# Seven-product stage: sums of the weights on VectorE, squares on ScalarE, earlier splits, and separate slots for the last pair

## The chip, the cores and the metric

One core of one Trainium2 chip runs the whole kernel. The metric is device time in microseconds (us) of one launch, the median of several runs. Beside the timed runs there is one profiled execution of the same program, and all rows below come from that one. The engines are called PE (TensorE), DVE (VectorE), ACT (ScalarE), POOL (GpSimd) and SP (SyncE, which here issues transfers).

## The reference

Three steps follow one another: a retention layer over (4, 8, 576, 64), a feed-forward layer with a softmax-like gate and a layer norm, and a second feed-forward layer with a squared ReLU. The change touches the third one alone, for the last 1536 of the 2304 tokens:

```python
def _moe2_ref(x, w_in, w_out):        # x 2304 x 512, w_in 512 x 2048, w_out 2048 x 512
    h = x @ w_in
    r = np.maximum(h, 0.0)
    g = r * r
    return (g @ w_out).astype(np.float32)
```

All data is float32. Each matrix factor is held as a high part (rounded to the type that PE multiplies at full rate) and a low part (the rest), and a product is the sum of high x high, high x low and low x high.

## The kernel before

The order of every engine's instructions is the order in which the code issues them. The first two steps, and the second feed-forward layer for the first two blocks of 384 tokens, are issued from the string ORDER. The rest is `seven()`: three blocks of 512 tokens, eight *pairs* of weight units for each, so 24 pairs, numbered n = 0 to 23. A unit is 128 columns of w_in with the 128 rows of w_out that belong to them, and both stay on the chip.

In a pair, PE computes two first-layer tiles (`m3s(2n)` and `m3s(2n+1)`, 12 products of 512 columns each, L452 to L454), both into the one PSUM bank `acc["m"]`, so the second starts only when ACT has read the first (the ReLU of L527). The squares of the two tiles are a matrix of 2 x 2 sub-blocks A11, A12, A21, A22; the matching rows of w_out are B11, B12, B21, B22. Their 2 x 2 product is formed with seven products in place of eight. The left factors are A11, A12, A22, S4 = A12 - S2, S1 = A21 + A22, S2 = S1 - A11 and S3 = A11 - A21; the right ones are B11, B21, B22 and the sums T1 to T4 of the weights. `products(n, fs)` issues the six PE instructions of each product f (L540 to L542, 256 columns each), into seven PSUM accumulators p0 to p6 that live over a block.

The other engines prepare the factors:

- `sums(n)` (L553 to L559) forms T1 to T4 from both parts of the weights, on POOL, into the one buffer `sums`; in the first block T1 is formed too and overwrites B12 in its unit.
- `m3s` squares the ReLU's output on DVE (L528). `forms(n)` (L563) makes S1 to S4 on DVE.
- `split(f)` is `hi_lo`: ACT writes the high part (L85), DVE subtracts it for the low part (L86). `later_parts()` splits T2, T3, T4 in one operation of 768 columns and then A22, S1, S2 and S3. There is one slot for each split factor, so a split of pair n waits until the products of pair n-1 have read the slot.
- `xb_split` (L442 on ACT, L443 on POOL) splits the next block's input, one chunk in each of the last four pairs of a block.
- `result` (L596 to L608) adds p0 to p6 into the four output quarters at a block's end, spread over the next block's first two pairs; `result_last` does it at the very end.

On PE the order of pair n is `m3s(2n)`, products 0 to 2 of pair n-1, `m3s(2n+1)`, products 3 to 6 of pair n-1. On ACT and DVE, `later_parts()` of pair n-1 stands behind the ReLU and the square of `m3s(2n)`, and `sums(n)` is issued behind `forms(n)`. After the last pair, `later_parts()` and the seven products of pair 23 remain.

Of the kernel before, what the change touches and what calls it, by code (L numbers as in the profile page):

```python
# [9 lines left out]
F32R = mybir.dt.float32r  # L10
# [25 lines left out]
def tile_retention_solu_relu2(  # L36
# [23 lines left out]
    nc = tc.nc  # L60
# [435 lines left out]

    LEFT = ["A11", "A12", "S4", "A22", "S1", "S2", "S3"]
    RIGHT = ["B11", "B21", "B22", "T4", "T1", "T2", "T3"]
    sq, wf, part = {}, {}, {}

    def seven_tiles():
        a = x2p.tile([P, 2, 6, HS], F32R, tag="x2_0", name="parts")
        r_ = [dec.tile([P, 4, HS], F32R, tag="raw", name=f"sums{x}", bufs=3) for x in "hl"]
        for n, f in enumerate(LEFT[:6]):
            part[f] = (a[:, 0, n], a[:, 1, n])
        part["S3"] = (r_[0][:, 3], r_[1][:, 3])
        part["T"] = (r_[0][:, 0:3], r_[1][:, 0:3])
        for n, f in enumerate(("T3", "T4", "T2")):
            part[f] = (r_[0][:, n], r_[1][:, n])
        wf["f"] = dec.tile([P, 4, HS], F32, tag="raw", name="sums", bufs=3)  # L510
        acc["m"] = bank("h", [P, TS], "m3", 2)
        for n in (0, 1, 3, 4, 5):
            acc["p", n] = r_bank([P, 2, HS], f"p{n}")
        acc["p", 2] = bank("s", [P, 2, HS], "p2", 1)
        acc["p", 6] = bank("h", [P, 2, HS], "p6", 2)

    def factor(f, p):
        if f in part:
            return part[f]
        u, w = {"B11": (0, 0), "T1": (0, 1), "B21": (1, 0), "B22": (1, 1)}[f]  # L520
        return [x[:, 1, w * HS:(w + 1) * HS] for x in units[2 * p + u]]

    def m3s(i, then=lambda j: None):
        b, c = divmod(i, KF2)
        first_layer(acc["m"], NJOINT + b, c, then)
        g = bw["p"].tile([P, TS], F32, tag="g" if i % 3 == 2 else "rl", name="g", bufs=1 if i % 3 == 2 else 2)
        nc.scalar.activation(g, acc["m"], AF.Relu)  # L527
        nc.vector.tensor_tensor(g, g, g, ALU.mult)  # L528
        r = "1" if i % 2 == 0 else "2"
        sq["A1" + r], sq["A2" + r] = g[:, :HS], g[:, HS:]  # L530

    def products(n, fs):
        p = n % (KF2 // 2)
        for f in fs:
            lh, ll = part[LEFT[f]]
            rh, rl = factor(RIGHT[f], p)
            for t in range(2):
                w = slice(t * P, (t + 1) * P)
                o = acc["p", f][:, t]
                nc.tensor.matmul(o, lh[:, w], rh, start=(p == 0 and t == 0), stop=False, skip_group_check=True)  # L540
                nc.tensor.matmul(o, lh[:, w], rl, start=False, stop=False, skip_group_check=True)  # L541
                nc.tensor.matmul(o, ll[:, w], rh, start=False, stop=(p == KF2 // 2 - 1), skip_group_check=True)  # L542

    def split(f):
        hi_lo(*part[f], sq[f])


    def sums(n):
        p = n % (KF2 // 2)
        f = wf["f"]  # L550
        (h0, l0), (h1, l1) = units[2 * p], units[2 * p + 1]
        v = lambda x: x[:, 1].bitcast(F32).rearrange("q (a b) -> q a b", a=2)
        nc.gpsimd.tensor_tensor(f[:, 0::3], v(h0), v(l0), ALU.add)  # L553
        nc.gpsimd.tensor_tensor(f[:, 1:3], v(h1), v(l1), ALU.add)
        if n < KF2 // 2:
            nc.gpsimd.tensor_tensor(f[:, 3], f[:, 3], f[:, 0], ALU.subtract)
            hi_lo(*factor("T1", p), f[:, 3])
        nc.gpsimd.tensor_tensor(f[:, 2], f[:, 2], f[:, 3], ALU.subtract)
        nc.gpsimd.tensor_tensor(f[:, 0:2], f[:, 2:3].to_broadcast([P, 2, HS]), f[:, 0:2], ALU.subtract)  # L559

    def form(f, tag, x, y, op):
        sq[f] = bw["p"].tile([P, HS], F32, tag=tag, name=f, bufs=2)
# [2 lines left out]
    def forms(n):  # L565
        form("S1", "gh", "A21", "A22", ALU.add)
        form("S2", "gl", "S1", "A11", ALU.subtract)
        form("S4", "gh", "A12", "S2", ALU.subtract)
        split("A12")
        split("S4")  # L570
        form("S3", "gl", "A11", "A21", ALU.subtract)

    def later_parts():
        hi_lo(*part["T"], wf["f"][:, 0:3])
        for f in "A22", "S1", "S2", "S3":
            split(f)


    def res_out(r, c):
# [53 lines left out]
    def seven():  # L633
        np_ = KF2 // 2
        end = NSEV * np_
        for n in range(end):
# [3 lines left out]

            nxt = None
            if p >= np_ - KD and b + 1 < NJOINT + NSEV:
                nxt = lambda j: xb_split(b + 1, p - np_ + KD, nc.gpsimd) if j == KD - 1 else None
            m3s(2 * n, nxt or (lambda j: None))
            if n == 0:
                m4(NJOINT * KF2 - 1)
                sums(0)
            else:
                if p == 1 and n > 1:
                    result(b - 1, 2)  # L650
                later_parts()
                products(n - 1, range(0, 2) if n == end - 1 else range(0, 3))
                if p == 0:
                    result(b - 1, 0)
            split("A11")
            m3s(2 * n + 1)
            if n == end - 1:
                products(n - 1, range(2, 3))
            forms(n)
            if n:  # L660
                sums(n)
                products(n - 1, range(3, 7))
                if p == 0:
                    result(b - 1, 1)
        n = end - 1
        later_parts()
        products(n, range(0, 3))
        result(b, 0)
        for k in 5, 4, 6, 3:
# [119 lines left out]
```

## Time and profile before

| what | value |
|---|---|
| timed runs: median (lowest to highest of 3) | 740.79 us (739.29 to 741.36) |
| the profiled execution's own time | 744.68 us |
| its span, first to last instruction | 742.7 us |
| PE busy | 697.0 us, 94% |
| DVE busy | 589.6 us, 79% |
| ACT busy | 356.9 us, 48% |
| POOL busy | 281.7 us, 38% |
| mean granted clock of PE | 0.991 of full speed |

The seven-product stage is the last 288 us of the span: its first PE instruction starts at 454.42 us. Busy shares are means over stages with different limits, so the stage has to be read by itself, pair by pair. PE's matmuls are pipelined and their ends are modelled, so that the distance between two starts tells more of PE than the duration of one.

### The profile page before, as it was taken

The page shows a single profiled execution, that of the slowest core. Times are in us where ns is not written, and L with a number is a line of the kernel's source. Part 1 is how long each engine was busy: PE and PEld are TensorE (multiplying, and loading weights), DVE is VectorE, ACT ScalarE, POOL GpSimd, SP SyncE. Part 2 cuts the span into 40 slices and gives each one's busy share as a digit, 9 for nine tenths or more (in the row PEclk, how much of TensorE's full clock was granted, in tenths as well). Part 3 has the DMA queues.
Part 4 walks back from the last instruction along what each step waited for, and adds up shares of the span by engine and source line. Part 5 has one row for each costly group of instructions (what it writes and reads, how often), then busy time and mean ns, then how long its engine had stood idle before and what let it go on. Part 6 is the DMA issues. An engine that isn't in the chain of part 4 may idle for free. (4 is left out here: it accounts for less than half of the span.)

```text
span 742.7 us, 12712 instructions
## 1 busy us (share of the span) xinstructions
PE 697.0 (94%) x4928; PEld 620.4 (84%) x4928; DVE 589.6 (79%) x963; ACT 356.9 (48%) x761; POOL 281.7 (38%) x243
## 2 busy tenths in 40 slices
PE   0879999999999999999999999999999999999993
PEld 0768889888989999999989897987887988879993
DVE  4658998674656477548978886999999999999995
ACT  2656784563344454545646555433434344333342
POOL 3475664210212021013232324457662564534540
PEclk9999999999999999999999999999999999999998
DMA  9999991200000001012333303000002000020002
GB/s 198 192 225 225 204 227 60 71 2 0 30 1 30 1 29 33 26 57 88 112 94 105 113 30 85 2 1 1 1 1 57 1 1 2 1 57 1 1 1 57
DMA packets 66029, 44.97 MB, mean 61 GB/s; under 512 B 40497, under 2 KB 61105, under 8 KB 65969
## 3 DMA queue, kind: packets, MB, share of 16 engines
q1 hardware_dynamic: 65808, 44.03, 25.2%
q8 instruction: 38, 0.62, 0.4%
q14 instruction: 23, 0.18, 0.1%
q10 hardware_dynamic: 160, 0.13, 0.1%
HBM read 39.44 MB, written 4.72 MB: 59 GB/s over the span
## 5 line engine op out<-in xcount | busy, mean ns | idle before, releaser
L452 PE MATMUL m<-xh,uh 128*128 128x512 f32 (+1 forms) x320 | 118.8, 371 | 1.2 <-ACT g L527 0.7
L453 PE MATMUL m<-xl,uh 128*128 128x512 f32 (+1 forms) x320 | 118.2, 369 | 0.1
L454 PE MATMUL m<-xh,ul 128*128 128x512 f32 (+1 forms) x320 | 117.8, 368 | 0.0
L86 DVE TENSOR_TENSOR parts<-S,parts 128x256 fp32r<-128x256 f32 x72 | 78.6, 1118 | 5.0 <-ACT parts L85 4.8
L419 PE MATMUL m<-lh,woh 128*128 128x256 f32 x288 | 82.3, 286 | 0.0
L420 PE MATMUL m<-ll,woh 128*128 128x256 f32 x288 | 81.5, 283 | 0.0
L421 PE MATMUL m<-lh,wol 128*128 128x256 f32 x288 | 81.5, 283 | 0.0
L161 POOL TENSOR_TENSOR x<-x 128x512 int32<-128x512 int32 x24 | 36.1, 1503 | 112.5 <-DVE x L160 104.6
L85 ACT ACTIVATE parts<-g 128x256 fp32r<-128x256 f32 x72 | 29.6, 411 | 99.4 <-DVE g L528 99.4
L553 POOL TENSOR_TENSOR sums<-uh,ul 128x512 f32<-128x512 f32 x24 | 33.6, 1402 | 105.3 <-DVE sumsl L86 105.3
L452 PEld LDWEIGHTS m<-xh,uh 128*128 128x128 f32 x320 | 60.4, 189 | 9.5 <-ACT g L527 2.4
L454 PEld LDWEIGHTS m<-xh,ul 128*128 128x128 f32 x320 | 60.1, 188 | 7.8
L453 PEld LDWEIGHTS m<-xl,uh 128*128 128x128 f32 x320 | 60.3, 189 | 7.1 <-DVE xl L443 0.5
L542 PE MATMUL p<-uh,parts 128*128 128x256 f32 x192 | 56.1, 292 | 2.0 <-DVE parts L86 1.7
L356 PE MATMUL h<-wih,xh 128*128 128x512 f32 x144 | 57.7, 401 | 0.2 <-DVE e L379 0.2
L357 PE MATMUL h<-wil,xh 128*128 128x512 f32 x144 | 56.3, 391 | 0.0
L358 PE MATMUL h<-wih,xl 128*128 128x512 f32 x144 | 56.3, 391 | 0.0
L419 PEld LDWEIGHTS m<-lh,woh 128*128 128x128 f32 x288 | 55.2, 192 | 0.6 <-issue 0.2
L420 PEld LDWEIGHTS m<-ll,woh 128*128 128x128 f32 x288 | 55.2, 192 | 0.4
L421 PEld LDWEIGHTS m<-lh,wol 128*128 128x128 f32 x288 | 55.2, 192 | 0.0
L540 PE MATMUL p<-uh,parts 128*128 128x256 f32 x192 | 54.5, 284 | 0.3 <-ACT parts L85 0.3
L541 PE MATMUL p<-ul,parts 128*128 128x256 f32 x192 | 54.5, 284 | 0.0
(137 smaller groups left out, 1891.8 us busy)
## 6 DMA issues: line engine op xcount, KB each, us to landing
raw<-in_moe_w_out_dram SPq DMA_DIRECT2D x24, 512.0 KB, 3.4
raw<-in_moe_w_in_dram SPq DMA_DIRECT2D x20, 512.0 KB, 3.8
k<-in_k_dram SPq DMA_DIRECT2D x16, 256.0 KB, 6.7
q<-in_q_dram SPq DMA_DIRECT2D x16, 256.0 KB, 6.8
v<-in_v_dram SPq DMA_DIRECT2D x16, 256.0 KB, 6.8
out_dram<-x SPq DMA_DIRECT2D x32, 128.0 KB, 2.4
raw<-in_moe_w_in_dram SPq DMA_DIRECT2D x8, 256.0 KB, 7.7
q<-in_q_dram SPq DMA_DIRECT2D x4, 128.0 KB, 6.0
```

The source lines that it names most:

```text
L86: nc.vector.tensor_tensor(l, src, h.bitcast(F32), ALU.subtract)
L356: nc.tensor.matmul(p_, h_[:, i], wi_h[i][:, cols], start=(i == 0), stop=False)
L357: nc.tensor.matmul(p_, h_[:, i], wi_l[i][:, cols], start=False, stop=False)
L358: nc.tensor.matmul(p_, l_[:, i], wi_h[i][:, cols], start=False, stop=(i == KD - 1))
L419: nc.tensor.matmul(p_, wo_h[i][:, w], h_[:, i], start=(i == 0), stop=False)
L420: nc.tensor.matmul(p_, wo_h[i][:, w], l_[:, i], start=False, stop=False)
L421: nc.tensor.matmul(p_, wo_l[i][:, w], h_[:, i], start=False, stop=(i == KF - 1))
L452: nc.tensor.matmul(p_, uh[:, 0, w], xh, start=(j == 0), stop=False)
L453: nc.tensor.matmul(p_, uh[:, 0, w], xl, start=False, stop=False)
L454: nc.tensor.matmul(p_, ul[:, 0, w], xh, start=False, stop=(j == KD - 1))
L540: nc.tensor.matmul(o, lh[:, w], rh, start=(p == 0 and t == 0), stop=False, skip_group_check=True)
L542: nc.tensor.matmul(o, ll[:, w], rh, start=False, stop=(p == KF2 // 2 - 1), skip_group_check=True)
```

## The change

The sums of the weights move from POOL to DVE, and so does the subtraction of `xb_split` in this stage; POOL is left without an instruction there. The square moves from DVE to ACT (Square in place of the multiplication). The sums of pair n are issued ahead of A11's split instead of behind the forms, and the later splits of pair n are issued at the end of pair n, ahead of the next pair's ReLU, instead of behind it. The last pair gets slots of its own for T2 to T4, A22, S1, S2 and S3 (in the buffers of the input's splits, which are free by then), and its sums are split ahead of `m3s(47)`.

```diff
+    def last_slots():
+        for i, fs in enumerate((("T3", "T4"), ("T2", "A22"), ("S1", "S2"), ("S3",))):
+            x = [bw["p"].tile([P, 2, HS], F32R, tag=f"x{y}{i}", name="slots", bufs=2) for y in "hl"]
+            for n, f in enumerate(fs):
+                last[f] = tuple(y[:, n] for y in x)
+            if i == 0:
+                last["T"] = [(*x, slice(0, 2)), (None, None, slice(2, 3))]
+        last["T"][1] = (*last["T2"], 2)
+
+    def slots(n):
+        return last if n == NSEV * KF2 // 2 - 1 else part
...
         nc.scalar.activation(g, acc["m"], AF.Relu)
-        nc.vector.tensor_tensor(g, g, g, ALU.mult)
+        nc.scalar.activation(g, g, AF.Square)
...
-        nc.gpsimd.tensor_tensor(f[:, 0::3], v(h0), v(l0), ALU.add)
-        nc.gpsimd.tensor_tensor(f[:, 1:3], v(h1), v(l1), ALU.add)
+        nc.vector.tensor_tensor(f[:, 0::3], v(h0), v(l0), ALU.add)
+        nc.vector.tensor_tensor(f[:, 1:3], v(h1), v(l1), ALU.add)
         if n < KF2 // 2:
-            nc.gpsimd.tensor_tensor(f[:, 3], f[:, 3], f[:, 0], ALU.subtract)
+            nc.vector.tensor_tensor(f[:, 3], f[:, 3], f[:, 0], ALU.subtract)
             hi_lo(*factor("T1", p), f[:, 3])
-        nc.gpsimd.tensor_tensor(f[:, 2], f[:, 2], f[:, 3], ALU.subtract)
-        nc.gpsimd.tensor_tensor(f[:, 0:2], f[:, 2:3].to_broadcast([P, 2, HS]), f[:, 0:2], ALU.subtract)
+        nc.vector.tensor_tensor(f[:, 2], f[:, 2], f[:, 3], ALU.subtract)
+        nc.vector.tensor_tensor(f[:, 0:2], f[:, 2:3].to_broadcast([P, 2, HS]), f[:, 0:2], ALU.subtract)
...
-                nxt = lambda j: xb_split(b + 1, p - np_ + KD, nc.gpsimd) if j == KD - 1 else None
+                nxt = lambda j: xb_split(b + 1, p - np_ + KD, nc.vector) if j == KD - 1 else None
             m3s(2 * n, nxt or (lambda j: None))
             if n == 0:
                 m4(NJOINT * KF2 - 1)
-                sums(0)
             else:
                 if p == 1 and n > 1:
                     result(b - 1, 2)
-                later_parts()
                 products(n - 1, range(0, 2) if n == end - 1 else range(0, 3))
                 if p == 0:
                     result(b - 1, 0)
-            split("A11")
+            sums(n)
+            split(n, "A11")
+            if n == end - 1:
+                last_slots()
+                split_sums(n)
             m3s(2 * n + 1)
             if n == end - 1:
                 products(n - 1, range(2, 3))
             forms(n)
             if n:
-                sums(n)
                 products(n - 1, range(3, 7))
                 if p == 0:
                     result(b - 1, 1)
+            if n < end - 1:
+                split_sums(n)
+            later_parts(n)
         n = end - 1
-        later_parts()
         products(n, range(0, 3))
         result(b, 0)
```

PE's instructions and their order stay as they are. What moves stands on ACT and DVE, and the rows below show it for the middle of the stage, around pair 10 of 0 to 23. `g` is the buffer of a ReLU's output and its square, S1 to S4 are the forms, `sums` the weights' sums, `parts` and `sumsh`/`sumsl` the split slots; lines above L500 have other numbers in the changed file.

ACT before, from the ReLU of `m3s(21)` (L527) to that of `m3s(23)`:

```order
L527 ACTIVATE g_6104<-m3_5007 128x512
L85 ACTIVATE parts_5003<-g_6104 128x256
L85 ACTIVATE parts_5003<-S4_6111 128x256
L527 ACTIVATE g_6159<-m3_5007 128x512
L85 ACTIVATE sumsh_5004<-sums_5006 128x768
L85 ACTIVATE parts_5003<-g_6104 128x256
L85 ACTIVATE parts_5003<-S1_6107 128x256
L85 ACTIVATE parts_5003<-S2_6109 128x256
L85 ACTIVATE sumsh_5004<-S3_6117 128x256
L85 ACTIVATE parts_5003<-g_6159 128x256
L527 ACTIVATE g_6204<-m3_5007 128x512
```

The splits of pair 10's T, A22, S1, S2 and S3 stand behind the ReLU of `m3s(22)`, the second L527. ACT in the change, from the ReLU of `m3s(21)` (L539, with the square L540 behind it) to that of `m3s(22)`:

```order
L539 ACTIVATE g_6108<-m3_5007 128x512
L540 ACTIVATE g_6108<-g_6108 128x512
L85 ACTIVATE parts_5003<-g_6108 128x256
L85 ACTIVATE parts_5003<-S4_6115 128x256
L85 ACTIVATE sumsh_5004<-sums_5006 128x768
L85 ACTIVATE parts_5003<-g_6108 128x256
L85 ACTIVATE parts_5003<-S1_6111 128x256
L85 ACTIVATE parts_5003<-S2_6113 128x256
L85 ACTIVATE sumsh_5004<-S3_6121 128x256
L539 ACTIVATE g_6169<-m3_5007 128x512
L540 ACTIVATE g_6169<-g_6169 128x512
```

The same five splits now stand directly behind A12's and S4's, and the ReLU of `m3s(22)` and its square come after them. DVE in the change, pair 10 (L565 to L571 the sums, L86 the low parts, L575 the forms):

```order
L565 TENSOR_TENSOR sums_5006<-uh4_3781,ul4_3782 128x2x256
L566 TENSOR_TENSOR sums_5006<-uh5_3783,ul5_3784 128x512
L570 TENSOR_TENSOR sums_5006<-sums_5006 128x256
L571 TENSOR_TENSOR sums_5006<-sums_5006 128x512
L86 TENSOR_TENSOR parts_5003<-g_6069,parts_5003 128x256
L575 TENSOR_TENSOR S1_6111<-g_6069,g_6108 128x256
L575 TENSOR_TENSOR S2_6113<-S1_6111,g_6069 128x256
L575 TENSOR_TENSOR S4_6115<-g_6108,S2_6113 128x256
L86 TENSOR_TENSOR parts_5003<-g_6108,parts_5003 128x256
L86 TENSOR_TENSOR parts_5003<-S4_6115,parts_5003 128x256
L575 TENSOR_TENSOR S3_6121<-g_6069 128x256
L86 TENSOR_TENSOR sumsl_5005<-sums_5006,sumsh_5004 128x768
```

Four sums stand at the head of the pair, and no square (L528) is left; behind the last row come the four low parts of A22, S1, S2 and S3, and then pair 11's sums.

## Rows read from the trace of the kernel before

**Rows 1.** The page, part 1: busy time, share and instructions of each engine.

```profile
PE 697.0 (94%) x4928; PEld 620.4 (84%) x4928; DVE 589.6 (79%) x963; ACT 356.9 (48%) x761; POOL 281.7 (38%) x243
```

**Rows 2.** Waits, 480 to 742.7 us: waiter <- awaited: us in total, times, longest.

```profile
ACT parts L85 <- DVE g L528: 95.1, 24, 7.1
...
PE p L542 <- DVE parts L86: 5.6, 13, 0.8
```

**Rows 3.** Busy time by stretches cut at the first PE instruction of a pair.

```profile
core 0: us, PE busy (x) PEld busy (x) DVE busy (x) ACT busy (x) POOL busy (x), PEclk, DMA share, GB/s
454.42:463.17 8.75, 8.00 (x34) 5.85 (x32) 4.78 (x9) 4.87 (x10) 0.53 (x1) 1.00 0.71 156
...
507.76:519.98 12.22, 11.59 (x69) 9.80 (x68) 11.60 (x16) 5.11 (x13) 8.04 (x7) 1.00 0.01 1
...
555.52:570.01 14.49, 12.88 (x68) 10.88 (x67) 14.11 (x22) 4.29 (x10) 5.31 (x5) 0.88 0.35 74
570.01:580.53 10.52, 10.52 (x68) 9.54 (x67) 10.16 (x15) 4.30 (x10) 5.12 (x5) 1.00 0.00 0
...
646.53:661.30 14.77, 13.02 (x68) 10.88 (x67) 14.39 (x23) 4.34 (x10) 5.24 (x5) 0.89 0.34 71
...
714.02:733.06 19.04, 16.71 (x109) 14.71 (x108) 17.74 (x31) 8.06 (x19) 5.04 (x5) 1.00 0.00 0
473.80:714.02 240.22, 232.81 (x1389) 204.94 (x1388) 230.39 (x317) 97.61 (x233) 124.93 (x103) 0.99 0.05 10
```

**Rows 4.** Timeline of pair 10: start, us, engine, line, operation, out<-in.

```profile
572.35 0.42 DVE L86 TENSOR_TENSOR parts<-g,parts 128x256 fp32r<-128x256 f32 x1
...
572.76 0.28 PE L540 MATMUL p<-uh,parts 128*128 128x256 f32 x1
...
574.91 0.40 PE L452 MATMUL m<-xh,uh 128*128 128x512 f32 x1
...
575.42 1.41 POOL L553 TENSOR_TENSOR sums<-uh,ul 128x512 f32<-128x512 f32 x1 [5.25 <-DVE sumsl L86]
575.59 2.95 DVE L86 TENSOR_TENSOR parts<-S,parts 128x256 fp32r<-128x256 f32 x2
...
576.79 1.47 POOL L554 TENSOR_TENSOR sums<-uh,ul 128x512 f32<-128x512 f32 x1
...
577.66 0.28 PE L540 MATMUL p<-sumsh,parts 128*128 128x256 f32 x1
```

**Rows 5.** Groups by line and shape, 480 to 742.7 us: busy us, mean ns.

```profile
L86 DVE TENSOR_TENSOR parts<-S,parts 128x256 fp32r<-128x256 f32 x68 | 74.8, 1127 | 4.6 <-ACT parts L85 4.6
...
L528 DVE TENSOR_TENSOR g<-g 128x512 f32<-128x512 f32 x43 | 39.6, 922 | 3.2 <-ACT g L527 3.1
...
L85 ACT ACTIVATE parts<-g 128x256 fp32r<-128x256 f32 x66 | 27.1, 411 | 95.1 <-DVE g L528 95.1
...
L527 ACT ACTIVATE g<-m 128x512 f32<-128x512 f32 x43 | 25.5, 593 | 31.1 <-PE m L454 30.9
...
L563 DVE TENSOR_TENSOR S<-g 128x256 f32<-128x256 f32 x44 | 18.6, 422 | 0.8
...
L85 ACT ACTIVATE sumsh<-sums 128x768 fp32r<-128x768 f32 x22 | 18.4, 834 | 0.0
```

**Rows 6.** The same view, pair 10 alone (570.01 to 580.53 us): DVE's squares.

```profile
L528 DVE TENSOR_TENSOR g<-g 128x512 f32<-128x512 f32 x2 | 1.4, 682 | 0.0
```

**Rows 7.** Timeline, pair 9, the second pair of a block: first product 3 of PE.

```profile
564.25 0.36 PE L540 MATMUL p<-sumsh,parts 128*128 128x256 f32 x1 [0.93 <-DVE x L608]
```

**Rows 8.** Timeline of the end: a waiting product, and the output's first and last additions.

```profile
729.37 0.39 PE L540 MATMUL p<-sumsh,parts 128*128 128x256 f32 x1 [0.40 <-ACT parts L85]
...
731.42 0.69 DVE L617 TENSOR_TENSOR x<-x,p 128x512 f32<-128x512 f32 x1
...
735.13 0.75 DVE L630 TENSOR_TENSOR x<-x,p 128x256 f32<-128x256 f32 x2
```

**Rows 9.** Timeline of the stage's start: the first product of pair 1.

```profile
463.17 0.50 PE L452 MATMUL m<-xh,uh 128*128 128x512 f32 x1 [0.69 <-ACT g L527]
```

More of the change, by code (lines that the diff above doesn't have):

```diff
@@ L498, in tile_retention_solu_relu2 @@
     RIGHT = ["B11", "B21", "B22", "T4", "T1", "T2", "T3"]
-    sq, wf, part = {}, {}, {}
+    sq, wf, part, last = {}, {}, {}, {}
     def seven_tiles():
@@ L506, in seven_tiles @@
         part["S3"] = (r_[0][:, 3], r_[1][:, 3])
-        part["T"] = (r_[0][:, 0:3], r_[1][:, 0:3])
         for n, f in enumerate(("T3", "T4", "T2")):
             part[f] = (r_[0][:, n], r_[1][:, n])
+        part["T"] = [(r_[0][:, 0:3], r_[1][:, 0:3], slice(0, 3))]
+        last.update(part)
         wf["f"] = dec.tile([P, 4, HS], F32, tag="raw", name="sums", bufs=3)
@@ L515, in seven_tiles @@
         acc["p", 6] = bank("h", [P, 2, HS], "p6", 2)
+    def last_slots():
[8 more added lines that the diff above has]
+        return last if n == NSEV * KF2 // 2 - 1 else part
     def factor(f, p):
-        if f in part:
-            return part[f]
         u, w = {"B11": (0, 0), "T1": (0, 1), "B21": (1, 0), "B22": (1, 1)}[f]
@@ L534, in products @@
         for f in fs:
-            lh, ll = part[LEFT[f]]
-            rh, rl = factor(RIGHT[f], p)
+            lh, ll = slots(n)[LEFT[f]]
+            rh, rl = slots(n).get(RIGHT[f]) or factor(RIGHT[f], p)
             for t in range(2):
@@ L542, in products, with split @@
                 nc.tensor.matmul(o, ll[:, w], rh, start=False, stop=(p == KF2 // 2 - 1), skip_group_check=True)
-    def split(f):
-        hi_lo(*part[f], sq[f])
+    def split(n, f):
+        hi_lo(*slots(n)[f], sq[f])
     def sums(n):
@@ L568, in forms, with split_sums, later_parts @@
         form("S4", "gh", "A12", "S2", ALU.subtract)
-        split("A12")
-        split("S4")
+        split(n, "A12")
+        split(n, "S4")
         form("S3", "gl", "A11", "A21", ALU.subtract)
-    def later_parts():
-        hi_lo(*part["T"], wf["f"][:, 0:3])
+    def split_sums(n):
+        for h, l, w in slots(n)["T"]:
+            hi_lo(h, l, wf["f"][:, w])
+    def later_parts(n):
         for f in "A22", "S1", "S2", "S3":
-            split(f)
+            split(n, f)
     def res_out(r, c):
```

## The prediction
> **What bounds the kernel now.** The page comes first: PE is busy for 94% of the span, DVE for 79%, POOL for 38% [rows 1]. That says only that PE is nearly full as a mean, so the stage that the change touches is read by itself. The waits of that stage come next: ACT stood for 95.1 us until DVE had squared a tile, and PE stood 13 times until DVE had written a low part [rows 2]. ACT's 95 us cost nothing as such; the PE row is the one to follow, because it says that where PE waits, it waits for DVE.
>
> How much PE waits is read by cutting the stage into pairs [rows 3]. Pair 10 lasts 10.52 us and PE has no gap in it, so 10.52 us is what a pair costs when PE alone sets the time. Pair 5, with T1 and an input split on POOL beside the sums, lasts 12.22 us, and the second pair of a new block lasts 14.49 or 14.77 us at a granted clock of 0.88 and 0.89. Pairs 2 to 22, 21 of them, take 240.22 us, while 21 x 10.52 is 220.92 us. So **19.30 us** of those pairs is PE standing still or running at the lower of its two clock levels, 1.2 GHz, after it stood. The last stretch takes 19.04 us, where a pair and seven more products without a gap would take 15.54 (10.52, and 2.15 + 2.87 for the products, from the starts in [rows 4]).
>
> Then the question is why DVE is late. It is busy for 10.16 of the 10.52 us of even the clean pair [rows 3], but not with work of its own: a subtraction of 256 columns takes 0.42 us when POOL is idle, and two of them took 2.95 us from 575.59, while POOL ran two sums from 575.42 to 578.26 [rows 4]. Over the stage the same subtraction averages 1127 ns, 68 times, and the square 922 ns [rows 5], against 422 ns for a form of equal size [rows 5] and 682 ns for a square where POOL rests [rows 6]. **A DVE operation that meets POOL ends about when POOL's does.**
>
> **The change, part by part.** All durations are of the profiled execution. Its own time, 744.68 us, is 3.89 us above the median of 740.79; I take the difference that the change makes as the same in both.
>
> *POOL leaves, the sums go to DVE.* DVE gains four sums in a pair: three of 512 columns at 0.68 us (priced as the square that POOL did not meet [rows 6]) and one of 256 at 0.42, together 2.46 us. It loses two squares, 2 x 0.68 = 1.36. Its other work at the undisturbed price is four forms and seven low parts of 256 columns, 11 x 0.42 = 4.62, and one low part of 768, at most three times 0.42 = 1.26. Sum: 2.46 + 4.62 + 1.26 = 8.34 us in 10.52. In the first block T1 adds 0.84, and in eight pairs the input's split adds 0.84 (or 0.68): 10.02 at most. So DVE fits, tightly in pairs 4 to 7.
>
> *Squares on ACT.* No row shows a Square of 512 columns here. The nearest is the ReLU of the same tile on the same engine, 593 ns [rows 5]; from below it could be no less than the 411 ns of a 256-column copy, from above the 834 ns of a 768-column one. I take 0.60. ACT's pair is then four times 0.60, seven copies at 0.41 and one of 0.83, 6.1 us: it fits.
>
> *Does the new order make PE wait?* I walk one pair from its start at 0. From [rows 3, 4], PE does the even tile from 0 to 2.75, products 0 to 2 to 4.90, the odd tile to 7.65, products 3 to 6 to 10.52. ACT reads the odd tile from about 7.85 to 8.45 and squares it to 9.05. DVE makes S1, S2, S4 by 10.4, the low parts of A12 and S4 by 11.3, S3 by 11.7. ACT's split of T waits for product 6 (10.52), which read the slot; T, A22, S1, S2 and S3 take it from 10.85 to 13.3. The next even tile ends at 13.27 and its ReLU may start at 13.47: ACT is just free, and even 1.3 us later the odd tile at 15.42 would not notice. DVE's low parts end by 14.7, the sums by 17.15, A11 by 17.6; the next forms may start at 19.6. PE needs S4 at 14.7 and has it at 11.3; it needs T and A22 at 18.17 and has them by 13.4. **No wait is left in an ordinary pair**, with 1.3 us spare on ACT and 2.0 on DVE (0.3 in pairs 4 to 7). Gain: the 19.30 us above, less the next item.
>
> *Block ends.* The result's additions stay on DVE: one before the sums, three of about 0.69 behind S3 (priced as the one at 731.42 [rows 8]), four (two of 0.69, two in 0.75) ahead of the next pair's sums. By the same walk S3 is ready at 11.7, three additions 13.75, five low parts 16.7, the last addition 18.85. PE's product 3 overwrites what that addition reads, and wants to at 18.17. Rows show durations that overlap, so this wait lies between 0 and the 0.93 of before [rows 7]; I take 0.4 at each of two block ends: -0.8.
>
> *Start.* The stage's first 8.75 us hold 7.6 us of PE work; 0.69 of the rest is PE waiting for a ReLU with one bank [rows 9], which stays. About 0.45 goes with POOL. New is that in pair 1 five splits stand ahead of the ReLU without seven products before them: 0 to 0.7 us. Net +0.2, between -0.3 and +0.5.
>
> *End.* Now the last splits wait for product 6 of pair 22 and PE stands, at 729.37 for one [rows 8]. With own slots and the sums split before `m3s(47)`, the walk gives all low parts by 12.6 us after the pair's start, when product 5 needs S2 at 12.7. The addition that waits for product 5 can start at 10.52 + 2.15 + 0.72 + 0.2 = 13.6; before it started at 731.42 - 714.02 = 17.4. Behind it the chain of additions is the same, 731.42 to 735.88. Gain 3.8, between 2.5 and 4.2.
>
> **Sum:** 19.3 - 0.8 + 0.2 + 3.8 = 22.5 us. The span goes from 742.7 to 720.2, the profiled time to 722.2, the median to 740.79 - 22.5 = **718.3 us**. With every bound at its best the gain is 19.3 + 0.5 + 4.2 = 24.0, 716.8; the runs before lie up to 1.5 below their median, hence 715.3 as the lower end.
>
> **The rivals.** *Block ends keep their stall.* The additions come as late as before and PE stands, then runs at the lower level: pairs 9 and 17 keep their 3.97 and 4.25 us over 10.52. The gain falls by 8.2 - 0.8 to 15.1: 725.7 us. For it: my walk leaves nothing spare there. Against: pair 5 stood too, and the clock stayed at 1.00 [rows 3]; and DVE's backlog at these ends was POOL's. Chance 0.11.
>
> *ACT becomes the late one.* Five splits wait for product 6 and hold the next ReLU behind them, and the odd tile waits for that ReLU in the one bank. It decides when the splits end 1.3 us later than walked, say if S3 is late or Square costs the upper bound. At 0.3 us beyond that in each of 21 pairs: -6.3, 724.6 us. Chance 0.08.
>
> *DVE becomes the bound: slower.* If the stretching of DVE's operations did not come from POOL, the 10.16 us of the clean pair would stay, less 1.36, plus the sums at the stage's stretched ratio (922/682 x 2.46 = 3.33): 12.13, and 0.36 between operations as now, 12.49 us a pair. 21 pairs then take 262.3 instead of 240.2: 22.1 us more, 762.9. It turns from gain to loss at 240.22 / 21 = 11.44 us of DVE a pair. Against it: the same operation at 0.42 and 1.47 within four microseconds, told apart only by POOL [rows 4]. Chance 0.03. The Trainium skill's "Perfetto Trace Analysis" (Optimizing Scalar/DVE Operations) speaks for this side: where DVE is saturated, work should go off it, to ScalarE or even GpSimd; by that advice bringing sums to an engine at 97% loses, towards the 762.9. The same section adds that GpSimd shares an SBUF read port with DVE, so that moving work between those two may gain nothing; the trace agrees with this second half [rows 4], and that is why I do not follow the first.
>
> *Nothing comes of it.* PE is full in clean pairs, and if the waits of the others had another source than DVE's lateness, they would stay: 740 us. The main row of PE's waits names DVE [rows 2]. Chance 0.02.
>
> **How the numbers follow.** My forecast has the remaining 0.76. The range 715.3 to 727.0 takes in the two slower but still winning rivals and leaves out the last two and their mixtures. Faster by over 0.3% (2.2 us, about what this measurement can tell) are the first three cases, 0.95; same 0.02; slower 0.03.
>
> **What would show it.** Right: POOL has no row in the stage; DVE's low parts average near 0.42 us; pairs 2 to 22 last 10.5 to 10.6 us, but for pairs 9 and 17 at most a microsecond more; from the last pair's start to the first addition behind product 5 is about 13.6 us; the granted clock stays 1.00. Wrong: DVE's 256-column operations still far over 0.42 (slower), a ReLU that starts late behind S3's split (ACT), or pairs 9 and 17 near 14 us.

## The result, and the profile after

The changed kernel takes 719.96 us (median of four runs, 718.66 to 720.62) beside 740.04 us for the kernel before (739.16 to 741.36): a ratio of 0.9725, with a 95% interval of 0.9703 to 0.9748. That is 20.1 us less, where 22.5 were forecast, and the time lies inside the range of 715.3 to 727.0. The profiled execution took 720.62 us with a span of 718.9 us, 24.1 us under the profiled one of before.

The first view is the busy time by stretches, cut as in [rows 3]: pair 0, pairs 2 to 22 together, pairs 5, 9, 10, 17 and 20, and the last pair. The columns are those of [rows 3].

```profile
453.97:462.29 8.32, 7.64 (x34) 6.00 (x32) 4.58 (x10) 5.48 (x13) 0.00 (x0) 1.00 0.71 158
473.10:694.02 220.92, 220.92 (x1389) 200.31 (x1387) 171.17 (x377) 127.27 (x275) 0.00 (x0) 1.00 0.05 10
504.66:515.18 10.52, 10.52 (x68) 9.54 (x67) 8.64 (x21) 6.55 (x16) 0.00 (x0) 1.00 0.01 2
546.74:557.26 10.52, 10.52 (x69) 9.54 (x67) 10.20 (x22) 5.69 (x12) 0.00 (x0) 1.00 0.29 61
557.26:567.78 10.52, 10.52 (x69) 9.54 (x67) 8.09 (x19) 5.57 (x13) 0.00 (x0) 1.00 0.19 41
630.90:641.42 10.52, 10.52 (x69) 9.54 (x67) 10.20 (x22) 5.68 (x12) 0.00 (x0) 1.00 0.29 62
662.46:672.98 10.52, 10.52 (x69) 9.54 (x67) 7.30 (x17) 5.68 (x13) 0.00 (x0) 1.00 0.01 2
694.02:709.46 15.44, 15.44 (x110) 14.46 (x108) 12.96 (x29) 9.48 (x21) 0.00 (x0) 1.00 0.00 1
```

Read the length of each stretch first: from pair 2 to pair 22 every pair takes 10.52 us, the two at block ends (9 and 17) too, and 21 pairs take 220.92 us, which is 21 x 10.52 exactly. PE has no gap in any of them and the granted clock is 1.00 throughout. The fifth busy column, POOL's, is zero. DVE's, the third, is 171.17 / 21 = 8.15 us as the mean of these pairs, where before it was 230.39 / 21 = 10.97. In an ordinary pair without a block end (pair 20) it is 7.30, where the clean pair of before had 10.16 [rows 3], although DVE now does the sums and gave away only the squares.

The second view shows why: groups by line and shape, from 460 us on, to be set against [rows 5].

```profile
L540 ACT ACTIVATE g<-g 128x512 f32<-128x512 f32 x47 | 29.7, 632 | 1.5
L86 DVE TENSOR_TENSOR parts<-g,parts 128x256 fp32r<-128x256 f32 x71 | 29.7, 418 | 0.0
...
L86 DVE TENSOR_TENSOR parts<-S,parts 128x256 fp32r<-128x256 f32 x70 | 27.5, 420 | 3.7 <-ACT parts L85 1.1
...
L575 DVE TENSOR_TENSOR S<-g 128x256 f32<-128x256 f32 x48 | 20.3, 422 | 40.4 <-ACT g L540 40.4
...
L566 DVE TENSOR_TENSOR sums<-uh,ul 128x512 f32<-128x512 f32 x23 | 15.7, 683 | 0.0
```

The low parts that averaged 1127 ns now average 420. A sum on DVE takes 683 ns, as the square that POOL did not meet did [rows 6]; the square on ACT takes 632 ns. DVE now stands idle ahead of the forms, 40.4 us in all, until ACT has squared a tile. It was the engine that others waited for, and it waits now.

Five rows of the timeline carry the ends: PE's only wait in the whole stage (pair 1's start), the additions at pair 9 with the product that overwrites what they read, and the last additions.

```profile
462.29 0.50 PE L452 MATMUL m<-xh,uh 128*128 128x512 f32 x1 [0.69 <-ACT g L539]
...
553.31 0.75 DVE L623 TENSOR_TENSOR x<-x,p 128x256 f32<-128x256 f32 x2
...
554.39 0.28 PE L552 MATMUL p<-sumsh,parts 128*128 128x256 f32 x1
...
707.62 0.69 DVE L632 TENSOR_TENSOR x<-x,p 128x512 f32<-128x512 f32 x1 [0.59 <-PE p L554]
...
711.31 0.75 DVE L645 TENSOR_TENSOR x<-x,p 128x256 f32<-128x256 f32 x2
```

### The profile page after: what moved, and what is told of

It reads as the page before. It is cut to its first block, busy times and chain, and to the rows that moved or that the text cites. A ratio compares the mean times of both kernels' runs of the same rounds, so it can differ in the third digit from the quotient of the medians.

```text
span 718.9 us, 12609 instructions
## 1 busy us (share of the span) xinstructions
PE 686.3 (95%) x4928; PEld 618.1 (86%) x4928; DVE 522.9 (73%) x1032; ACT 390.9 (54%) x810; POOL 139.9 (19%) x127
## 4 chain that ended last, share of the span: by engine, by line
PE 90%; DMA 4%; DVE 3%; ACT 1%; issue 1%; SPq 0%; DVEq 0%; ACTq 0%
PE m L452 9%; PE m L453 9%; PE m L454 9%; PE p L554 6%; PE p L553 5%; PE p L552 5%; PE m L419 5%; PE m L421 5%; PE m L420 5%; PE h L356 4%; PE h L357 4%; PE h L358 4%; PE acc L482 3%; PE acc L483 3%; PE acc L481 3%; DMA raw<-in_moe_w_in_dram 3%
## 5 line engine op out<-in xcount | busy, mean ns | idle before, releaser
L539 ACT ACTIVATE g<-m 128x512 f32<-128x512 f32 x48 | 28.7, 598 | 64.7 <-PE m L454 64.5
L554 PE MATMUL p<-uh,parts 128*128 128x256 f32 x190 | 53.8, 283 | 0.0
L552 PE MATMUL p<-uh,parts 128*128 128x256 f32 x190 | 53.6, 282 | 0.0
L575 DVE TENSOR_TENSOR S<-g 128x256 f32<-128x256 f32 x48 | 20.3, 422 | 40.4 <-ACT g L540 40.4
L362 DVE TENSOR_REDUCE mx<-h 128x1 f32<-128x512 f32 x36 | 24.5, 687 | 31.3 <-PE h L358 31.0
```

## The experiments

The theory to test: a two-input operation of DVE is held while POOL runs one, so that POOL's sums made DVE late and DVE made PE wait. The rival: PE was freed by the sooner order of issue, and by the last pair's own slots. Each expectation below says what this means for its run, and so what its theory A, theory B or rival is. The runs' medians scatter by a few microseconds, and in the profiles of one and the same kernel most of this lies ahead of the stage (see the last section). So each kernel is also judged by its *stage*: from the first PE instruction of `m3s(0)` to the end of the span, in its profiled execution. The kernel before has 742.7 - 454.42 = 288.28 us, the changed one 718.9 - 453.97 = 264.93. Spans are shown to 0.1 us, so differences of stages are good to about 0.1 us.

| kernel | stage, us | against the changed one | median, us | ratio to before (95% interval) |
|---|---|---|---|---|
| before, first and second profile | 288.28, 287.67 | +23.4, +22.7 | | 1 |
| changed, three profiles | 264.93, 264.95, 265.01 | 0 | 719.96, 721.73, 719.27 | 0.9725 (0.9703 to 0.9748) |
| engines alone | 271.13 | +6.2 | 726.86 | 0.9774 (0.9727 to 0.9822) |
| order alone | 301.79 | +36.9 | 758.24 | 1.0193 (1.0141 to 1.0246) |
| sums on POOL | 272.96 | +8.0 | 727.92 | 0.9784 (0.9743 to 0.9825) |
| squares on DVE | 266.47 | +1.5 | 721.84 | 0.9711 (0.9666 to 0.9756) |
| idle work on POOL | 306.38 | +41.5 | 761.29 | 1.0245 (1.0228 to 1.0262) |
| shared slots at the end | 265.98 | +1.1 | 721.26 | 0.9693 (0.9670 to 0.9716) |
| stores on two queues, second bank | 263.23 | -1.7 | 719.33 | 0.9670 (0.9627 to 0.9712) |
| both ends | 262.56 | -2.4 | 717.48 | 0.9649 (0.9632 to 0.9665) |

Each ratio sets a kernel's runs beside runs of the kernel before taken with them. The changed kernel's is that of its first runs; its other two were 0.9703 and 0.9688. The first column has short names for the sections below.

### Engines alone

The kernel before with the change's engines alone; its order and its slots stay:

```diff
-        nc.vector.tensor_tensor(g, g, g, ALU.mult)
+        nc.scalar.activation(g, g, AF.Square)
...
-        nc.gpsimd.tensor_tensor(f[:, 0::3], v(h0), v(l0), ALU.add)
+        nc.vector.tensor_tensor(f[:, 0::3], v(h0), v(l0), ALU.add)
... (the other sums likewise)
-                nxt = lambda j: xb_split(b + 1, p - np_ + KD, nc.gpsimd) if j == KD - 1 else None
+                nxt = lambda j: xb_split(b + 1, p - np_ + KD, nc.vector) if j == KD - 1 else None
```

> The kernel before with the engines of the change alone: sums and input splits on DVE, squares on ACT, in the old order of issue and with the old shared slots at the end. Theory A (POOL stretches DVE's operations; with POOL silent DVE has 8.3 us of work in a pair of 10.52): DVE's 256-column low parts average 0.42 us, ordinary pairs last 10.5 us, pairs 4 to 7 at most 0.4 us more; the end keeps one to three of the 3.8 us, the block ends a microsecond or two; time 721 to 726 us. Theory B (the order of issue is what freed PE): the later splits still stand behind the ReLU and the sums behind the forms, so PE waits nearly as before and the time stays at 733 us or more.

Measured: 17.2 us of the 23.4 of the stage come with the engines alone, the time being just above the forecast span of theory A. The rows of the stretch from 480 us (within pair 2) to the end of pair 22, of the two block ends (pairs 9 and 17), and of the last pair:

```profile
480.00:697.83 217.83, 216.99 (x1356) 195.73 (x1355) 168.11 (x370) 123.31 (x271) 0.00 (x0) 1.00 0.05 11
548.46:560.10 11.64, 11.22 (x69) 9.59 (x67) 11.28 (x25) 5.73 (x13) 0.00 (x0) 1.00 0.32 68
633.74:645.23 11.49, 11.07 (x68) 9.58 (x67) 11.13 (x24) 5.72 (x13) 0.00 (x0) 1.00 0.33 71
697.83:718.92 21.09, 17.99 (x109) 16.59 (x108) 16.45 (x34) 9.02 (x20) 0.00 (x0) 0.87 0.00 1
```

PE is idle for 0.84 us in 218 us (two waits of 0.42 us, one at each block end). The block ends last 11.64 and 11.49 us, 2.1 us too many together; every other pair from 2 to 22 lasts 10.52. So ordinary pairs need nothing but the new division of engines. The last pair, though, takes 21.09 us to the last product, 2.05 more than before [rows 3] and 5.65 more than in the changed kernel. Its waits name one row:

```profile
PE p L540 <- ACT parts L85: 2.5, 1, 2.5
```

One product stood 2.5 us behind ACT's splits, and the clock of that stretch fell to 0.87. A silent POOL brings nothing at the end as long as sums and splits are issued late, as they are here.

### Order alone

The changed kernel with the old engines: the same lines as above, turned round.

```diff
-        nc.scalar.activation(g, g, AF.Square)
+        nc.vector.tensor_tensor(g, g, g, ALU.mult)
...
-        nc.vector.tensor_tensor(f[:, 0::3], v(h0), v(l0), ALU.add)
+        nc.gpsimd.tensor_tensor(f[:, 0::3], v(h0), v(l0), ALU.add)
... (the other sums likewise)
-                nxt = lambda j: xb_split(b + 1, p - np_ + KD, nc.vector) if j == KD - 1 else None
+                nxt = lambda j: xb_split(b + 1, p - np_ + KD, nc.gpsimd) if j == KD - 1 else None
```

> The changed kernel with the old engines: sums and input splits on POOL, squares on DVE, but the sooner order of sums and splits and the last pair's own slots. Theory A (POOL stretches DVE): DVE's low parts still average about 1 us, DVE is busy for 10 us of a pair, pairs 4 to 7 stay near 12 us; only the end gains 2 to 3 us; time 733 to 741 us. Theory B (the order is what freed PE): pairs fall to 10.6 us although DVE's operations are still stretched; time at most 725 us.

Measured: 758.24 us, slower than before and slower than either theory said. The order that belongs to the gain is a loss of 13.5 us of stage without the engines. The waits of the stage and the two pairs at the block ends (the columns are those of [rows 2] and [rows 3]):

```profile
PE p L552 <- DVE x L623: 11.6, 2, 5.8
...
PE m L452 <- ACT g L539: 10.1, 14, 1.8
```

```profile
559.70:578.34 18.64, 12.83 (x66) 11.39 (x67) 16.76 (x28) 5.02 (x12) 4.92 (x4) 0.82 0.25 52
578.34:588.84 10.50, 10.50 (x68) 9.53 (x67) 8.66 (x10) 3.99 (x9) 4.99 (x4) 1.00 0.05 10
654.66:673.58 18.92, 13.11 (x66) 11.67 (x67) 16.75 (x28) 5.02 (x12) 4.92 (x4) 0.82 0.26 54
```

These are two of the prediction's rivals, at work. Product 3 waited 5.8 us, twice, for the last addition of the result, which now stands behind five low parts that POOL stretches; each time the clock fell (0.82 in the stretch). And first-layer tiles waited 14 times for a ReLU, which now stands on ACT behind the five splits. The ordinary pair behind the block end is clean, 10.50 us, with POOL at work, while pairs 2 to 8 last 11.2 to 14.4 us: as before, what POOL costs it costs where DVE has little to spare. The last pair, with its own slots, takes 19.21 us from its first to its last product (727.03 to 746.24), where it took 19.04 before [rows 3].

### The weights' sums alone back on POOL

`sums(n)` as before, everything else as in the change:

```diff
-        nc.vector.tensor_tensor(f[:, 0::3], v(h0), v(l0), ALU.add)
+        nc.gpsimd.tensor_tensor(f[:, 0::3], v(h0), v(l0), ALU.add)
... (the other sums likewise)
```

> The changed kernel with the weights' sums alone back on POOL; squares stay on ACT, input splits on DVE, order and slots as in the change. DVE's own work is then 5.9 us in a pair, POOL's 5.1 (5.9 in the first block). Theory A in its strong form (any work of POOL in the stage makes PE wait): DVE is stretched by about 4 us a pair, the block ends stall again; time 728 us or more. Theory A in its weak form (POOL costs only where it meets DVE work that PE waits for): POOL runs in the gap in which DVE waits for the next odd tile's square, A11's low part and a few others are stretched, PE waits nowhere but perhaps at block ends; time 719 to 723 us.

Measured: 8.0 us more stage, between the two forms. The first block end (pair 9), the pair behind it and the second block end (pair 17):

```profile
544.68:557.78 13.10, 10.79 (x69) 9.46 (x68) 12.47 (x22) 6.10 (x13) 4.99 (x4) 1.00 0.22 47
557.78:568.30 10.52, 10.52 (x69) 9.54 (x68) 7.80 (x10) 5.38 (x12) 5.01 (x4) 1.00 0.21 43
631.42:646.01 14.59, 12.28 (x68) 10.95 (x67) 12.46 (x22) 6.09 (x13) 4.98 (x4) 0.88 0.30 63
```

The pair between takes 10.52 us with 5.01 us of POOL in it, and so does every pair from 2 to 22 but the block ends and pair 18 (10.49): the weak form holds there. The block ends take 13.10 and 14.59 us, 2.6 and 4.1 too many, because product 3 again waits for the last addition (4.6 us in two waits), and the second time the clock falls with it. So, once the squares are on ACT and the order is new, moving the sums to DVE is needed for the block ends and not for ordinary pairs. The rest is 0.8 us at the start (pair 2 starts 471.04 - 451.14 = 19.90 us after the stage's start, 19.13 in the changed kernel) and 0.6 us from pair 23's start to the end of the span.

### The squares alone back on DVE

```diff
-        nc.scalar.activation(g, g, AF.Square)
+        nc.vector.tensor_tensor(g, g, g, ALU.mult)
```

> The changed kernel with the squares alone back on DVE, POOL silent. DVE has 9.7 us of work in an ordinary pair of 10.52, 11.4 us in pairs 4 to 7. Theory A (DVE's own work is what counts once POOL is silent): ordinary pairs still last 10.52 us, pairs 4 to 7 run up a backlog of under 4 us that DVE's spare of about 3 us for the next products mostly takes, and the block ends, with 4.9 us of additions on top, stand for 1 to 3 us each; time 720 to 727 us. Rival (ACT's squares gave nothing, DVE has room): exactly the changed kernel's 720 us, no wait of PE at a block end.

Measured: 1.5 us more stage; by the medians no difference that can be told. The second row is a block end's:

```profile
451.93:718.40 266.47, 255.74 (x1594) 230.34 (x1592) 230.92 (x488) 117.85 (x274) 0.00 (x0) 0.99 0.08 19
544.88:556.02 11.14, 10.78 (x68) 9.45 (x67) 10.79 (x23) 4.00 (x9) 0.00 (x0) 1.00 0.26 55
```

A block end takes 0.62 us too many (11.14 - 10.52; the other 0.56), less than the 1 to 3 us of theory A, and pairs 4 to 7 take 10.52. With POOL silent, DVE had room for the squares, and this part of the change is worth 1.5 us of stage, 1.2 of it at the block ends. The parts do not add up: the sums alone put back cost 8.0 us and the squares alone 1.5, but sums, squares and the input's split together 36.9 (order alone). The input's split was not put back by itself.

### Work on POOL that nobody needs

Four additions on POOL in each pair from the third on, into a region that nothing reads; no other engine waits for their result:

```diff
+    def idle_work():
+        f = wf["f"]
+        for k in range(KD):
+            nc.gpsimd.tensor_tensor(x2[1][:, k, 0:TS].rearrange("p (a b) -> p a b", a=2), f[:, 0:2], f[:, 2:4], ALU.add)
...
             sums(n)
+            if n > 1:
+                idle_work()
             split(n, "A11")
```

> The changed kernel with four additions of 512 columns on POOL in each pair from the third on, behind the pair's sums: they read the sums' buffer and write a region that nothing reads, so no engine waits for their results. Theory A (POOL stretches DVE whether or not its result is needed): POOL's 5.6 us a pair fall on the forms and the low parts behind them, these average 0.8 to 1.4 us in place of 0.42, S3 gets late, the next ReLU behind it too, and pairs last 11 to 12 us: 735 to 750 us. Rival (DVE was late in the kernel before because it waited for POOL's results, not because its operations were held): DVE's operations keep 0.42 us and the time stays at 720 us.

Measured: 761.29 us, 41.5 us more stage, beyond the 750 of theory A; the rival falls. Groups by shape, then the timeline of one pair:

```profile
L576 POOL TENSOR_TENSOR x<-sums 128x512 f32<-128x512 f32 x78 | 109.7, 1435 | 160.5 <-DVE sums L571 160.5
...
L580 DVE TENSOR_TENSOR S<-S,g 128x256 f32<-128x256 f32 x21 | 28.4, 1352 | 0.7
```

```profile
589.22 0.42 DVE L86 TENSOR_TENSOR parts<-g,parts 128x256 fp32r<-128x256 f32 x1
589.44 5.65 POOL L576 TENSOR_TENSOR x<-sums 128x512 f32<-128x512 f32 x4 [5.70 <-DVE sums L571]
590.04 1.04 DVE L580 TENSOR_TENSOR S<-g 128x256 f32<-128x256 f32 x1 [0.40 <-ACT g L540]
591.11 1.40 DVE L580 TENSOR_TENSOR S<-S,g 128x256 f32<-128x256 f32 x1
592.55 1.40 DVE L580 TENSOR_TENSOR S<-g,S 128x256 f32<-128x256 f32 x1
593.86 1.51 DVE L86 TENSOR_TENSOR parts<-g,parts 128x256 fp32r<-128x256 f32 x1
...
595.30 0.41 DVE L86 TENSOR_TENSOR parts<-S,parts 128x256 fp32r<-128x256 f32 x1
```

POOL's four additions run without a break from 589.44 to 595.09, and in that time DVE gets four operations done, one for each. Ahead of it and behind it the same kinds take 0.42 and 0.41 us. No engine waits for these additions, so this is no wait for data: **while POOL runs two-input operations one after the other, DVE gets one operation in for each of them, if it reads both its inputs from SBUF** (the on-chip memory of the tiles; PE's accumulators lie in PSUM). In 21 of the 22 pairs with this work, four operations of DVE start during POOL's four. The condition is shown by the run with the sums on POOL, at its first block end:

```profile
551.81 0.96 DVE L86 TENSOR_TENSOR sumsl<-S,sumsh 128x256 fp32r<-128x256 f32 x1
552.57 1.34 POOL L571 TENSOR_TENSOR sums<-sums 128x512 f32<-128x512 f32 x1
552.69 0.67 DVE L619 TENSOR_TENSOR x<-x,p 128x512 f32<-128x512 f32 x1
553.29 0.67 DVE L620 TENSOR_TENSOR x<-x,p 128x512 f32<-128x512 f32 x1
```

The low part, of 256 columns, took 0.96 us, where it takes 0.42 with a silent POOL; POOL ran a sum then too (from 551.68 to 552.49 us). The two additions of the result, of 512 columns each, read one input from PSUM (`p`). They took 0.67 us each beside a single operation of POOL, where with a silent POOL they take 0.68. The mechanism was forecast, with too wide a condition and too low a price. A reason for the price that fits the rows, though it was not tried by itself, is that the held operations are the forms: ACT's splits stood for 91.6 us until forms were ready, where in the changed kernel it was 24.9, and through the splits PE's products and the next ReLU came late.

### Shared slots at the end

The changed kernel without `last_slots`, its sums split at the usual place:

```diff
-        return last if n == NSEV * KF2 // 2 - 1 else part
+        return part
...
-                last_slots()
-                split_sums(n)
+                pass
...
-            if n < end - 1:
-                split_sums(n)
+            split_sums(n)
```

> The changed kernel without the last pair's own slots: its later splits wait for product 6 of pair 22 in the shared slots, its sums are split at the usual place. Theory A (3.8 us of the gain belong to the last pair's slots): 2.5 to 4.5 us more, the last product 3.5 us later, with one or more waits of PE behind the splits and the lower clock level after them. Rival (the end's gain came from POOL's silence, the slots hide what is hidden anyway): under 1 us more.

Measured: about 1 us more stage (265.98 beside 264.93), so theory A's number falls, and the rival's limit of 1 us lies within the reading. One wait of PE is left, 0.54 us, and no fall of the clock:

```profile
705.09 0.39 PE L554 MATMUL p<-sumsh,parts 128*128 128x256 f32 x1 [0.54 <-DVE parts L86]
```

But the rival's reason falls too. From the last pair's first to its last product there are 19.04 us before, 21.09 with the engines alone, 16.22 here and 15.44 with the whole change. Engines alone and this run both have a silent POOL and shared slots; what differs is the order, so the sooner order is worth 4.9 us there. POOL need not be silent for it, as the last pair's rows of order alone, of the sums on POOL and of the squares on DVE show:

```profile
727.03:746.24 19.21, 16.63 (x107) 14.77 (x108) 17.56 (x31) 8.14 (x20) 4.98 (x4) 1.00 0.00 0
698.58:714.45 15.87, 15.70 (x110) 14.52 (x108) 14.29 (x25) 9.14 (x21) 5.00 (x4) 1.00 0.00 0
693.34:708.78 15.44, 15.44 (x109) 14.46 (x108) 14.12 (x32) 8.06 (x19) 0.00 (x0) 1.00 0.00 1
```

All three have the sooner order and the own slots. Among them the gain is lost only where POOL's sums and DVE's squares come together (19.21 us, DVE busy for 17.56 of them); the sums on POOL alone leave 15.87. The slots add the last microsecond.

### The stage's two ends

Two edits at first: the last stores half from ACT's queue, and the stage's second first-layer tile in product 6's bank.

```diff
-                store(b, 0, t)
+                store(b, 0, t, eng=(nc.sync, nc.scalar)[t])
...
-                store(b, 1, t, slice(1, 2))
+                store(b, 1, t, slice(1, 2), (nc.sync, nc.scalar)[t])
...
-        first_layer(acc["m"], NJOINT + b, c, then)
+        m = acc["p", 6].rearrange("q a b -> q (a b)") if i == 1 else acc["m"]
+        first_layer(m, NJOINT + b, c, then)
...
-        nc.scalar.activation(g, acc["m"], AF.Relu)
+        nc.scalar.activation(g, m, AF.Relu)
```

> The changed kernel with two edits at the stage's two ends: the last stores are issued half from SP and half from ACT (six each, where SP issued ten), and the second first-layer tile of the stage goes into the bank that product 6 uses later, so that the third need not wait for the second one's ReLU. If the tail is SP's issuing (10 issues in 6.4 us behind the first addition, then 2.5 us to land), it gets 2 to 3 us shorter, and the start 0.7 us: 716 to 718 us beside 720. If the tail is the transfers' own time, nothing but the 0.7 us.

Measured: 1.7 us less stage. The stores did that (from pair 23's start to the end of the span 24.9 us became 23.2); the bank did nothing (pair 2 starts 19.15 us after the stage's start, 19.13 in the changed kernel), since the next tile now waited longer for the next ReLU, which stands behind pair 0's five splits:

```profile
468.18 0.50 PE L452 MATMUL m<-xh,uh 128*128 128x512 f32 x1 [0.89 <-ACT g L540]
```

The third edit puts these splits, for pair 0 alone, behind that ReLU:

```diff
+                if n == 1:
+                    split_sums(0)
+                    later_parts(0)
                 products(n - 1, range(0, 2) if n == end - 1 else range(0, 3))
...
-            if n < end - 1:
+            if 0 < n < end - 1:
                 split_sums(n)
-            later_parts(n)
+            if n:
+                later_parts(n)
```

> The changed kernel with the last stores on two queues, the stage's second first-layer tile in product 6's bank, and, for pair 0 alone, the later splits behind the next ReLU instead of ahead of it. Before this third edit the wait of 0.69 us only moved: from the ReLU of the second tile to that of the third, which stood behind the five splits (0.89 us). If ACT's order is what the third waits for, both waits go now, and the stage is 1 us shorter than with two edits and 2.7 us shorter than the changed kernel's 264.9; if the splits are then late for the products behind, PE waits there instead and nothing is gained.

> The changed kernel beside the one with both ends edited, on the same chip: 719 to 723 us, its stage 264.9 us in the profile whatever the time ahead of it is.

Measured: 2.4 us less stage than the changed kernel, where 2.7 were expected: pair 2, behind the splits that moved, takes 10.95 us. The median is 717.48 us beside 719.27 on the same chip. The ratios to before, 0.9649 (0.9632 to 0.9665) and 0.9688 (0.9666 to 0.9710), are barely apart. Of PE's waits in the stage one of 0.3 us, of a weight load, is left. The stores' issue, in the timeline of the changed kernel and of this one:

```profile
709.92 6.40 SPq L603 DMA_DIRECT2D out_dram<-x  x10
```

```profile
708.66 4.46 SPq L604 DMA_DIRECT2D out_dram<-x  x6
708.66 4.75 ACTq L604 DMA_DIRECT2D out_dram<-x  x6
```

Ten issues in a row from SP lasted to 716.32, 4.3 us beyond the last addition; six from each queue last to 713.41, 2.6 us beyond it (its last addition ends at 710.81). By its stage this is the shortest version; by the medians its lead over the changed kernel is barely clear.

## Why the prediction was right, point by point

| term | forecast | measured in the profiled executions |
|---|---|---|
| pairs 2 to 22 | -19.3 | 240.22 to 220.92: -19.30 |
| block ends, part of those pairs | +0.8 | 0 |
| start, to the first instruction of pair 2 | -0.2 | 473.80 - 454.42 = 19.38 to 473.10 - 453.97 = 19.13: -0.25 |
| end, from pair 23's start to the last addition | -3.8 | 735.88 - 714.02 = 21.86 to 712.06 - 694.02 = 18.04: -3.8 |
| sum | -22.5 | the stage -23.4; the span -23.8, of which 0.45 lies ahead of the stage |

**What bounds the kernel** was read rightly: the clean pair's 10.52 us is what PE needs, and all else was waiting. **DVE's load** was forecast at 8.34 us for an ordinary pair, which was too much: pair 20 shows 7.30. Its 16 operations add up to 8.07 us, since the low part of 768 columns takes 0.96 us and not 1.26, and independent operations overlap (two low parts of 0.42 us start at 664.52 and 664.86).

**The cause** was read rightly, and shown directly by the idle work on POOL. The rule in bold, that a DVE operation which meets POOL ends about when POOL's does, was too wide: it holds for operations with both inputs in SBUF, not for the result's additions (0.67 us beside POOL's 1.34).

The Trainium skill's "Perfetto Trace Analysis" (Optimizing Scalar/DVE Operations) says that GpSimd and DVE share an SBUF read port. The held operations agree with that. It adds that offloading between those two "might not help"; here, the other way round, bringing the sums from POOL to DVE gained 8.0 us of stage. It also says that it may make sense to take work off a saturated DVE, to ScalarE or even GpSimd. The squares moved to ScalarE gained 1.5 us with a silent POOL, so that part agrees; the sums left on GpSimd would have kept the 8.0 us in the kernel.

**The block ends** were mis-sized, 0.8 us instead of none. The walk put the last addition's end at 18.85 us after the pair's start and PE's product 3 at 18.17; measured from 536.22, pair 8's start, they are 17.84 (553.31 + 0.75) and 18.17 (554.39). The walk added durations, and DVE's independent operations start sooner than that: the additions of 0.68 us start 0.60 apart (552.00 and 552.60, profile of the changed kernel). 0.33 us were spare. The runs with the sums on POOL and with the squares on DVE show how little that is: both stand here first.

**The start** came out by both its parts: pair 0 is 0.43 us shorter without POOL (8.75 to 8.32), and pair 1, with five splits ahead of its ReLU, 0.18 longer (10.63 to 10.81).

**The end** came out as forecast, its first addition at 707.62 - 694.02 = 13.6 us after the pair's start. Where the prediction put that gain was only half right. It named the slots and the early sums; the slots are worth about 1 us, the sooner order 4.9 us with a silent POOL, and nothing while POOL's sums and DVE's squares come together. (The 15.54 us set beside the last stretch of before run to the end of the last product and the stretch to its start; to the start it would be 15.42, and 15.44 was measured.)

**The step that failed**, beside the block ends' term, is the sentence that the difference would be the same in the profile and in the medians. It was 24.1 us between the two profiled executions and 20.1 between the medians taken with them. In the two later sets of runs with both kernels, the medians differ by 21.9 (743.64 and 721.73) and 23.6 us (742.90 and 719.27). The stage repeats within 0.1 us in three profiles of the changed kernel and within 0.6 in two of before; the median does not. So how near 718.3 came to 719.96 is in part luck, and the terms of the sum are tested by the stage.

**The rivals** had their chances for a kernel in which the parts come together, and none of them happened there. Taken apart, two of them do: order alone has both the waiting block ends and the waiting ReLU, and is slower than before.

## What to carry to other kernels

When an engine is busy all the time, compare the same operation's duration with and without its neighbour at work before taking work off it: here DVE became free although it got more work than it gave away (2.46 us of sums a pair for 1.36 of squares, by the prediction's prices), because waiting for POOL was what filled it. What a new order of issue and a new division of engines are worth does not add up: here the engines alone took 17.2 us off the stage, the order with the slots alone put 13.5 on, and together they took 23.4 off. So test them in both combinations. And judge a change of one stage by the length of the stage, when what lies ahead of it scatters by more than the effect.

## What the runs showed that was not expected

**An order that gains with one division of engines loses with the other.** Issuing later splits ahead of the next ReLU cost 13.5 us of stage as long as POOL stretched DVE, most of it at two block ends, where one late addition of DVE stood for 5.8 us of PE and a fall of the clock behind it.

**Most of the scatter lies ahead of the stage.** A second profile of the kernel before and more runs of the changed one were made for that:

> A second profile of the kernel before. If what differs between its runs lies ahead of the stage, the stage takes 288.3 us again, within 0.5, and the start of the stage moves by a few us; if its own waits vary, pairs 2 to 22 take another time than 240.2 us.

> The changed kernel once more, beside the runs of this call, for its spread: 718 to 723 us, ordinary pairs of 10.52 us in the profile. If the gain of 24 us between the two profiled executions and of 20 us between the medians differ because the kernel before varies and the changed one does not, its runs lie within 2 to 3 us of one another while those of the kernel before spread over 5 us or more.

In the second profile of the kernel before the stage took 287.67 us, 0.6 under the first and just beyond the 0.5 that was expected, and pairs 2 to 22 took 239.57. Its span is 2.1 us shorter, and 1.5 of these lie ahead of the stage. The three spans of the changed kernel differ by up to 1.9 us, of which all but 0.1 lies ahead of it. The guess that the kernel before varies more than the changed one did not hold (742.82 to 744.72 beside 720.71 to 722.87). The stage's start lies between 447.92 and 455.87 us in the profiles of this study, with the same instructions ahead of it but for pair 0's sums. The first 100 us of four of them, before twice and the changed kernel twice:

```profile
0.00:100.00 100.00, 75.06 (x944) 62.51 (x944) 72.15 (x115) 58.63 (x121) 53.91 (x54) 1.00 1.03 209
```

```profile
0.00:100.00 100.00, 77.49 (x976) 64.44 (x976) 76.66 (x117) 60.42 (x123) 55.42 (x56) 1.00 1.06 213
```

```profile
0.00:100.00 100.00, 74.40 (x936) 61.43 (x936) 69.97 (x113) 58.73 (x120) 52.94 (x54) 1.00 1.05 208
```

```profile
0.00:100.00 100.00, 73.58 (x934) 61.47 (x936) 69.76 (x113) 59.09 (x120) 54.29 (x55) 1.00 1.05 207
```

PE has done between 934 and 976 products by 100 us, with the transfers' share at 1.03 to 1.06 in each. So some of the scatter is there already, while the inputs are loaded. The count does not order the stage's starts (936 products and a start at 454.05 us, 944 and 454.42), so more comes later; what makes one execution run ahead of another was not tried.
